# Head pairs' scores alternate in four of eight chunks, the gate's normalisation runs in steps between expert products, and second weight blocks load into other buffers

## The chip, the cores and the metric

The program runs on one core of a Trainium2 chip, in one launch. A time is the device's time for the whole program in microseconds (us), and lower is better. The engines are named as in the profile: PE (matrix products; PEld is its loading of stationary operands), DVE (vector), ACT (scalar), POOL (GpSimd), and SP, whose queue issues every DMA of this kernel.

## What is computed

The reference is an attention in blocks, then a gated feed-forward layer, then a layer of 8 experts that every token passes, weighted by a normalised gate. Cut to what matters:

```python
for c in range(768 // 32):                      # 4 x 8 heads, head size 64
    scores = scale * q_c @ k_full.T             # 32 queries, 8 memory keys + up to 56 keys around them
    a = softmax(scores); out[c] = a @ v_full
x = out.reshape(3072, 512)
x = (sigmoid(x @ w_gate) * (x @ w_val)) @ w_out # 512 -> 1536 -> 512
logits = x @ w_gate2; P = exp(logits - logits.max())       # 3072 x 8
for _ in range(8):                              # the gate's normalisation
    P /= P.sum(1, keepdims=True) + 1e-09
    P /= P.sum(0, keepdims=True) + 1e-09
    P *= N / E
out = sum(P[:, e:e+1] * (np.maximum(x @ w1[e], 0) @ w2[e]) for e in range(8))  # 512 -> 1024 -> 512
```

## The kernel before

Each large product is made of three: an operand is split into a high part (`h`) and a low part (`l`, the remainder, by `operand`, line 109: a copy on ACT, then a subtraction on POOL or DVE), and high x high, high x low and low x high are added in PSUM. Many of them are put together from seven products of half-size blocks (the names `p`, `chain`, `other`, `right`) in place of eight.

**Attention** (`attention`, line 183) works on chunks `c` of 384 tokens, 0 to 7, and on pairs of heads `hp`, 0 to 3. A pair's two heads `j` lie in partitions 0 to 63 and 64 to 127 of one tile. For each head four blocks of scores (`sc`, line 210: 64 rows of contraction, into one PSUM bank for each head), row maxima (`nm`) and exponentials with sums (line 229); chunks 0 to 3 (`PEM`) add the mask by a product on PE (line 207), chunks 4 to 7 by DVE (line 224). Then POOL scales by the sums' reciprocals, PE transposes (`pt`, line 244), and PE makes the weighted sums (`po`, line 257): four blocks for head 0 into partitions 0 to 63 of a bank, four for head 1 into 64 to 127. Outside of the first chunk all of `sc`, `pt` and `po` share two banks (`ps_a`). These products are of plain float32, and the profile records each of those of `sc` and `po` as two.

`attention` is a generator: its steps are put between the products of the feed-forward layer by a list of due places (`schedule`, `hook`). That layer runs on chunk pairs; its results go to memory (`x2d`), and the gate's logits stay on the chip.

**Experts** (the second half of `moe_chain`): the tokens go in three sets `s` of 1024, and for each set the units are (expert `e`, half `hf` of the 1024 hidden columns), each in two parts `fp`. `layer1` makes the hidden activations of a unit from `w1` (products `p`), and `layer2` the outputs from `w2` (`py` in set 0, `pzr` and `pzq` later). In set 0 the weights come raw from memory: `r1` (line 730) and `r2` (line 681), 512 KB each, both in the two buffers of tag `r` (`pair`, line 103). They are split into operands on the chip (`w1_operands`, nine tiles of tag `ws` for them; `w2_get`), and the operands are stored to memory for the later sets (`w1k`, line 144; `w2k`, lines 684 and 685). `sinkhorn` (line 608) normalises the gate `P`: in eight rounds, DVE sums and scales rows, PE sums columns by a product with ones (`pc`, line 629), DVE scales columns. Expert 0 of set 0 adds up unscaled, and is scaled by `P` when expert 1 begins (line 830).

The order of instructions is not that of the code alone. The program is written in program order, and `tile.TileContext(nc, schedule_with_timeline_sim=True)` then orders each engine's instructions when the program is built; each engine works through its own list strictly in that order. What an instruction waits for comes from the tiles that it reads and from buffers that come free.

## Time and profile before

| what | value |
|---|---|
| three runs | 2811.1, 2811.91, 2813.43 us; median 2811.91 |
| the profiled execution | 2814.29 us, its span 2812.5 us |
| PE, PEld | busy 96% and 86% of the span |
| DVE, ACT, POOL | busy 70%, 42%, 34% |
| memory | 562 MB moved, 200 GB/s on average |

The profiled execution is 2.4 us above the runs' median; the 1.8 us outside its span are start and end. A busy share is an average over very different stages: attention with the feed-forward layer reaches to about 820 us, and the first result of set 0 of the experts is stored at 1515.9 us.

### The profile page before, as it was taken

Reading aid. Unit: us, or ns where it says so; the run is one execution under the profiler, and the core shown is the slowest. Engines: PE = TensorE matmul, PEld = TensorE weight load, DVE = VectorE, ACT = ScalarE, POOL = GpSimd, SP = SyncE. Lnnn points to the kernel's source line nnn. Section 1 sums busy time; section 2 is a strip of 40 time slices with the busy share of each in tenths; the row PEclk is TensorE's granted clock in tenths of the full one; section 3 lists DMA queues with packets and bytes.
Section 4 is the critical chain, followed back from the end, with each engine's and each line's share of the span. In section 5 each row is a group of like instructions: output and inputs, shape, how many; then the busy total and the mean of one; then the engine's idle time right before and its main releaser. Section 6 shows DMA issues by size and latency. Waiting matters only on the chain.

```text
span 2812.5 us, 43343 instructions
## 1 busy us (share of the span) xinstructions
PE 2713.2 (96%) x15567; PEld 2405.6 (86%) x15567; DVE 1972.2 (70%) x3150; ACT 1189.9 (42%) x2564; POOL 970.0 (34%) x731
## 2 busy tenths in 40 slices
PE   7899999999987999999999999999998999999999
PEld 5798898999975888778877889999998899899998
DVE  8796666556576655554557798888888677667776
ACT  5565775655353333333333343433434433333332
POOL 4334774011043333333333243433434322233222
PEclk9899999999998999999999999999999999999999
DMA  5453667565654565565566566667665655555454
GB/s 201 139 177 125 241 238 244 189 201 176 204 186 169 184 213 180 176 209 177 180 207 233 178 236 220 210 225 248 239 215 184 239 192 182 203 214 214 175 183 187
DMA packets 256323, 562.04 MB, mean 200 GB/s; under 512 B 26889, under 2 KB 43785, under 8 KB 256108
## 3 DMA queue, kind: packets, MB, share of 16 engines
q1 hardware_dynamic: 256108, 559.27, 57.7%
q8 instruction: 123, 2.02, 0.3%
q14 instruction: 92, 0.75, 0.1%
HBM read 383.00 MB, written 176.16 MB: 199 GB/s over the span
## 4 chain that ended last, share of the span: by engine, by line
PE 78%; DVE 8%; DMA 5%; issue 3%; ACT 2%; POOL 2%; SPq 0%; POOLq 0%; DVEq 0%; ACTq 0%
PE p L743 9%; PE p L744 9%; PE p L745 9%; PE pzq L845 4%; PE pzq L844 4%; PE pzq L846 4%; DMA r<-in_wb 4%; PE py L76 3%; PE py L77 3%; PE py L78 3%; PE pzr L844 3%; PE pzr L845 3%; PE pzr L846 3%; PE px L77 2%; PE px L76 2%
## 5 line engine op out<-in xcount | busy, mean ns | idle before, releaser
L743 PE MATMUL p<-xh,w 128*128 128x512 f32 x1344 | 528.0, 396 | 23.4 <-ACT ce L765 12.8
L744 PE MATMUL p<-xl,w 128*128 128x512 f32 x1344 | 527.6, 393 | 0.1
L745 PE MATMUL p<-xh,w 128*128 128x512 f32 x1344 | 523.2, 392 | 1.4 <-POOL w L111 1.4
L743 PEld LDWEIGHTS p<-xh,w 128*128 128x128 f32 x1344 | 254.2, 189 | 76.6 <-ACT ce L765 19.5
L745 PEld LDWEIGHTS p<-xh,w 128*128 128x128 f32 x1344 | 253.7, 189 | 52.9 <-POOL w L111 3.1
L744 PEld LDWEIGHTS p<-xl,w 128*128 128x128 f32 x1344 | 254.4, 189 | 44.1 <-DVE xl L111 0.5
L111 POOL TENSOR_TENSOR gl<-ce,gh 128x512 fp32r<-128x512 f32 x64 | 88.2, 1378 | 545.7 <-ACT gh L110 545.7
L814 DVE SCALAR_TENSOR_TENSOR acc<-pzr,logit,acc 128x512 f32<-128x512 f32 (+1 forms) x362 | 201.0, 572 | 92.8 <-PE pzr L846 91.8
L814 DVE SCALAR_TENSOR_TENSOR acc<-pzq,logit,acc 128x512 f32<-128x512 f32 x244 | 176.7, 746 | 54.1 <-PE pzq L846 50.9
L77 PE MATMUL py<-w2b,gh 128*128 128x512 f32 x528 | 206.4, 391 | 0.0
L76 PE MATMUL py<-w2a,gh 128*128 128x512 f32 x528 | 205.9, 391 | 0.0
L78 PE MATMUL py<-w2a,gl 128*128 128x512 f32 x528 | 201.7, 391 | 0.0
L720 ACT ACTIVATE gh<-ca 128x512 fp32r<-128x512 f32 x96 | 60.6, 631 | 270.6 <-PE pzr L845 131.4
L111 POOL TENSOR_TENSOR sl<-cb,sh 128x512 fp32r<-128x512 f32 (+1 forms) x64 | 87.1, 1362 | 254.5 <-ACT sh L110 244.7
L111 POOL TENSOR_TENSOR w2b<-r,w2a 128x1024 fp32r<-128x1024 f32 x32 | 78.0, 2437 | 266.9 <-ACT w2a L110 266.9
L748 DVE TENSOR_TENSOR cd<-p,ce 128x512 f32<-128x512 f32 x96 | 65.8, 686 | 130.2 <-ACT ce L765 130.1
L844 PE MATMUL pzr<-w2c,sh 128*128 128x256 f32 x504 | 143.1, 284 | 3.7 <-DVE acc L814 3.3
L237 POOL TENSOR_TENSOR sm<-sm,rs 96x512 f32<-96x512 f32 x64 | 78.8, 1250 | 194.8 <-DVE rs L235 149.0
L845 PE MATMUL pzr<-w2d,sh 128*128 128x256 f32 x504 | 142.9, 284 | 0.0
L846 PE MATMUL pzr<-w2c,sl 128*128 128x256 f32 x504 | 141.2, 284 | 0.0
L814 DVE SCALAR_TENSOR_TENSOR acc<-py,logit,acc 128x512 f32<-128x512 f32 x116 | 84.9, 747 | 71.3 <-PE py L78 70.9
L111 POOL TENSOR_TENSOR w<-wq,w 128x512 fp32r<-128x512 f32 x64 | 87.0, 1360 | 88.5 <-ACT w L110 80.1
(288 smaller groups left out, 7824.7 us busy)
## 6 DMA issues: line engine op xcount, KB each, us to landing
w<-w1k SPq DMA_DIRECT2D x448, 256.0 KB, 4.5
w1k<-w SPq DMA_DIRECT2D x224, 256.0 KB, 4.0
r<-in_wb SPq DMA_DIRECT2D x96, 512.0 KB, 5.4
w2a<-w2k SPq DMA_DIRECT2D x64, 512.0 KB, 5.0
w2b<-w2k SPq DMA_DIRECT2D x64, 512.0 KB, 6.2
w_g<-wak SPq DMA_DIRECT2D x84, 256.0 KB, 3.5
w_v<-wak SPq DMA_DIRECT2D x84, 256.0 KB, 3.7
u<-in_qkv SPq DMA_DIRECT2D x28, 704.0 KB, 5.4
```

What stands on the lines that cost most here:

```text
L76: nc.tensor.matmul(ps, wh, xh, start=first, stop=False)
L77: nc.tensor.matmul(ps, wh, xl, start=False, stop=False)
L78: nc.tensor.matmul(ps, wl, xh, start=False, stop=last)
L111: return eng.tensor_tensor(out=l, in0=src, in1=h.bitcast(F32), op=ALU.subtract)
L237: nc.gpsimd.tensor_tensor(out=prob[j], in0=prob[j], in1=rs[:, j, :, None].to_broadcast([QB, NBLK, 128]), op=ALU.mult)
L743: nc.tensor.matmul(ps, wh[:, ks], xh, start=kk == 0 and not more, stop=False, skip_group_check=True)
L744: nc.tensor.matmul(ps, wh[:, ks], xl, start=False, stop=False, skip_group_check=True)
L745: nc.tensor.matmul(ps, wl[:, ks], xh, start=False, stop=kk == 1, skip_group_check=True)
L814: nc.vector.scalar_tensor_tensor(out=dst, in0=src, scalar=pe, in1=dst, op0=ALU.mult, op1=ALU.add)
L844: nc.tensor.matmul(ps, gh[:, cs], wh, start=fp == 0 and not more, stop=False, skip_group_check=True)
L845: nc.tensor.matmul(ps, gh[:, cs], wl, start=False, stop=False, skip_group_check=True)
L846: nc.tensor.matmul(ps, gl[:, cs], wh, start=False, stop=fp == 1, skip_group_check=True)
```

## The change

Five things are done, and each engine's list is then ordered anew:

- In chunks 4 to 7 the score products of a pair's two heads are written in turn (head 1, head 0, then 0, 1, 0, 1, 0, 1), with both banks open, and both heads' exponentials stand in one step of the generator. Chunks 0 to 3 keep their order.
- The weighted sums alternate between the heads in all chunks.
- In chunks 0 to 3 the maxima are scaled by ACT, no longer by DVE (`nm`, 32 small instructions).
- `sinkhorn` becomes a generator, moved on by every second call of `beat`, which stands ahead of each product of `layer1` and each `py` of `layer2`; what is left of it runs ahead of the third unit.
- `r2` in set 0 is no longer one block of 512 KB in a buffer of tag `r`, but two of 256 KB in buffers of tags `sh` and `sl`, which hold activations and have eight buffers each. Its copy on ACT and its subtraction on POOL are made in two halves.

```diff
--- before.py
+++ after.py
@@ -199,16 +199,27 @@
             first = c % 2
             nm = at.tile([QB, 2, NBLK], F32, tag="nm", name=f"nm{c}_{hp}")
             rs = at.tile([QB, 2, NBLK], F32, tag="rs", name=f"rs{c}_{hp}")
+            scb = [psum(f"sc{c}_{hp}_{j}")[:QB] for j in range(2)]
+
+            def score(j, b):
+                p0 = 64 * j
+                return nc.tensor.matmul(blocks(scb[j])[:, b, :], qT[p0:p0 + 64, b * QB:(b + 1) * QB],
+                                        kv[p0:p0 + 64, b, :], start=c not in PEM, stop=True, skip_group_check=c in PEM)
+
+            if c not in PEM:
+                ahead_of = score(1, 0)
+                with tc.issue_after(ahead_of.ins):
+                    score(0, 0)
+                    for b in range(1, NBLK):
+                        for j in range(2):
+                            score(j, b)
             for j in range(2):
-                p0 = 64 * j
-                scb = psum(f"sc{c}_{hp}_{j}")[:QB]
-                sc = blocks(scb)
+                sc = blocks(scb[j])
                 if c in PEM:
-                    nc.tensor.matmul(scb, mon, mro[:, first:first + NBLK].rearrange("p b q -> p (b q)"),
+                    nc.tensor.matmul(scb[j], mon, mro[:, first:first + NBLK].rearrange("p b q -> p (b q)"),
                                      start=True, stop=False, skip_group_check=True)
-                for b in range(NBLK):
-                    nc.tensor.matmul(sc[:, b, :], qT[p0:p0 + 64, b * QB:(b + 1) * QB],
-                                     kv[p0:p0 + 64, b, :], start=c not in PEM, stop=True, skip_group_check=c in PEM)
+                    for b in range(NBLK):
+                        score(j, b)
                 if lead:
                     sm = slot("v", f"sm{c}_{hp}_{j}")
                 else:
@@ -216,7 +227,7 @@
                 sm = blocks(sm[:QB])
                 if c in PEM:
                     nc.vector.tensor_reduce(out=nm[:, j], in_=sc, axis=AX.X, op=ALU.max)
-                    nc.vector.tensor_scalar(out=nm[:, j], in0=nm[:, j], scalar1=-0.125, scalar2=None, op0=ALU.mult)
+                    nc.scalar.mul(nm[:, j], nm[:, j], -0.125)
                     src, scale = sc, 0.125
                 else:
                     if not masked:
@@ -229,8 +240,10 @@
                     nc.scalar.activation(sm[:, b, :], src[:, b, :], AF.Exp, bias=nm[:, j, b:b + 1],
                                          scale=scale, accum_out=rs[:, j, b:b + 1])
                 prob.append(sm)
-                if j == 0:
+                if j == 0 and c in PEM:
                     yield
+            if c not in PEM:
+                yield
             nc.vector.tensor_scalar(out=rs, in0=rs, scalar1=1e-9, scalar2=None, op0=ALU.add)
             nc.vector.reciprocal(rs, rs)
             for j in range(2):
@@ -252,8 +265,8 @@
             yield
             po = psum(f"po{c}_{hp}")[:, 0:CT]
             pv = blocks(po)
-            for j in range(2):
-                for b in range(NBLK):
+            for b in range(NBLK):
+                for j in range(2):
                     nc.tensor.matmul(pv[64 * j:64 * j + 64, b, :], vv[:, b, j, :], pT[j][:, b, :],
                                      start=True, stop=True)
             if c < 2:
@@ -608,10 +621,12 @@
         def sinkhorn():
             m1 = sk.tile([128, 1], F32, tag="m1", name="m1")
             nc.vector.tensor_reduce(out=m1, in_=logit.rearrange("p n e -> p (n e)"), axis=AX.X, op=ALU.max)
+            yield
             pm = ps_y.tile([128, 512], F32, tag="y", name="pm")[0:1, 0:128]
             nc.tensor.transpose(pm, m1, ident)
             m2 = sk.tile([1, 1], F32, tag="m2", name="m2")
             nc.vector.tensor_reduce(out=m2, in_=pm, axis=AX.X, op=ALU.max)
+            yield
             pb = ps_y.tile([128, 512], F32, tag="y", name="pb")[:, 0:1]
             nc.tensor.matmul(pb, ones[0:1, :].to_broadcast([1, 128]), m2, start=True, stop=True)
             ng = sk.tile([128, 1], F32, tag="ng", name="ng")
@@ -625,6 +640,7 @@
                 nc.vector.tensor_tensor(out=P, in0=P, in1=r[:, :, None].to_broadcast([128, NN, E]), op=ALU.mult)
                 cs = sk.tile([128, E], F32, tag="cs", name=f"cs{i}")
                 nc.vector.tensor_reduce(out=cs, in_=P.rearrange("p n e -> p e n"), axis=AX.X, op=ALU.add)
+                yield
                 pc = ps_y.tile([128, 512], F32, tag="y", name=f"pc{i}")[:, 0:E]
                 nc.tensor.matmul(pc, ones.to_broadcast([128, 128]), cs, start=True, stop=True)
                 cr = sk.tile([128, E], F32, tag="cr", name=f"cr{i}")
@@ -632,6 +648,15 @@
                 nc.vector.reciprocal(cr, cr)
                 nc.vector.tensor_scalar(out=cr, in0=cr, scalar1=float(NT // E), scalar2=None, op0=ALU.mult)
                 nc.vector.tensor_tensor(out=P, in0=P, in1=cr[:, None, :].to_broadcast([128, NN, E]), op=ALU.mult)
+                if i % 2:
+                    yield
+
+        balance, beats = sinkhorn(), [0]
+
+        def beat():
+            beats[0] += 1
+            if beats[0] % 2:
+                next(balance, None)
 
         SW = 512
         SHB = 8
@@ -678,9 +703,10 @@
             raw = wb[e, hf, fp, :, :, 1, :]
             dh, dl = w2_tile(nm, "a"), w2_tile(nm, "b")
             if s == 0:
-                r = pair(f"r2_{nm}")
-                nc.sync.dma_start(out=r, in_=raw)
-                operand(dh, dl, nc.gpsimd, flat(r))
+                for f, k in enumerate(("sh", "sl")):
+                    r = gg.tile([128, 512], F32, tag=k, name=f"r2{k}_{nm}", bufs=SHB)
+                    nc.sync.dma_start(out=r, in_=raw[:, f, :])
+                    operand(dh[:, f * 512:(f + 1) * 512], dl[:, f * 512:(f + 1) * 512], nc.gpsimd, r)
                 nc.sync.dma_start(out=kept[0], in_=dh.bitcast(F32))
                 nc.sync.dma_start(out=kept[1], in_=dl.bitcast(F32))
                 return w2_sets(dh, dl)
@@ -737,6 +763,7 @@
                     return ps_h.tile([128, 512], F32, tag="h", name=f"p{i}_{nm}")
 
                 def product(i, ps, more=False):
+                    beat()
                     for kk in range(2):
                         ks = slice(kk * 128, (kk + 1) * 128)
                         (wh, wl), xh, xl = w[i], xop[i][0][kk], xop[i][1][kk]
@@ -820,6 +847,7 @@
 
             n_p = pairs(s, e, hf)
             for t in [h * 4 + j for j in range(n_p, 4) for h in range(2)]:
+                beat()
                 py = ps_y.tile([128, DM], F32, tag="y", name=f"py{s}_{e}_{hf}_{t}")
                 tt = slice((t % 4) * 128, (t % 4) * 128 + 128)
                 for fp in range(2):
@@ -881,7 +909,6 @@
                     each(f)
 
         xop = x_operands(0)
-        sinkhorn()
         work = [(s, e, hf) for s in range(NSB) for e in range(E) for hf in range(2)]
         gs, w2 = {}, []
         cur = layer1(0, 0, 0, xop, gs, w2)
@@ -889,6 +916,9 @@
         for n, (s, e, hf) in enumerate(work):
             for _ in cur:
                 pass
+            if n == 2:
+                for _ in balance:
+                    pass
             if e == 0 and hf == 0:
                 acc = [slot("v", f"acc{s}_{t}") for t in range(NTT)]
             args = (s, e, hf, gs, w2, acc)
```

The lists as the program is built show the following.

On PE, in chunk 7, where head pair 2's scores (`sc_2_0` for head 0, `sc_2_1` for head 1) and head pair 1's transposes stand, before:

```order
L76 MATMUL px_3_0_2_7250<-gh_3_0_0_7003,hwo_3_0_6756 128x384
L210 MATMUL sc_2_0_6910<-u_2_6906 96x128 x4
L244 MATMUL pt_1_0_6938<-ident,sm_1_0_6709 128x96 x4
...
L77 MATMUL px_3_1_1_7274<-gl_3_0_1_7085,hwo_3_0_6756 128x384
L244 MATMUL pt_1_1_6945<-ident,sm_1_1_6818 128x96 x4
L210 MATMUL sc_2_1_6968<-u_2_6906 96x128 x4
L78 MATMUL px_3_1_1_7274<-gh_3_0_1_7084,lwo_3_0_6757 128x384
```

and now:

```order
L206 MATMUL sc_2_1_6911<-u_2_6906 96x128
L206 MATMUL sc_2_0_6910<-u_2_6906 96x128 x2
L206 MATMUL sc_2_1_6911<-u_2_6906 96x128
L206 MATMUL sc_2_0_6910<-u_2_6906 96x128
L206 MATMUL sc_2_1_6911<-u_2_6906 96x128
L206 MATMUL sc_2_0_6910<-u_2_6906 96x128
L206 MATMUL sc_2_1_6911<-u_2_6906 96x128
...
L257 MATMUL pt_1_0_6950<-ident,sm_1_0_6714 128x96 x4
L257 MATMUL pt_1_1_6957<-ident,sm_1_1_6721 128x96 x4
```

Each head's run of four stood alone, with 24 products between the two runs; now the eight are one run in which the heads alternate, and the two transposes follow each other. This holds for 12 of the 16 pairs of chunks 4 to 7; in pairs 0 and 1 of chunks 4 and 6 the heads' runs still stand apart. Of the 24 groups of weighted sums in chunks 2 to 7, 13 stand as one run that alternates, and in 11 the first product stands apart from the other seven.

On SP, at the start of the experts (`r_0_0_0_1` is the second part's `r1`, then its `r2`; `w2b` is the last operand made from an `r2`), before:

```order
L684 DMA w2k_0_0_0_416<-w2a_0_0_0_9731 128x1024
L144 DMA w1k_0_0_4_196<-w_0_0_0_0_4_9635 128x512
L685 DMA w2k_0_0_1_417<-w2b_0_0_0_9732 128x1024
L731 DMA r_0_0_0_1_9739<-in_wb 128x2x512
L144 DMA w1k_0_0_5_197<-w_0_0_0_0_5_9636 128x512
L144 DMA w1k_0_0_6_198<-w_0_0_0_0_6_9637 128x512
L682 DMA r_0_0_0_1_9843<-in_wb 128x2x512
```

and now:

```order
L144 DMA w1k_0_0_5_197<-w_0_0_0_0_5_9513 128x512
L144 DMA w1k_0_1_0_199<-w_0_0_0_1_0_9654 128x512
L144 DMA w1k_0_0_6_198<-w_0_0_0_0_6_9514 128x512
L757 DMA r_0_0_1_0_9802<-in_wb 128x2x512
L144 DMA w1k_0_1_1_200<-w_0_0_0_1_1_9655 128x512
...
L144 DMA w1k_0_1_6_205<-w_0_0_0_1_6_9660 128x512
L757 DMA r_0_0_1_1_10091<-in_wb 128x2x512
...
L144 DMA w1k_1_0_4_210<-w_0_0_1_0_4_9808 128x512
L708 DMA r2sh_0_0_0_9642<-in_wb 128x512
L708 DMA r2sl_0_0_0_9646<-in_wb 128x512
```

Before, each `r1` is issued behind the store of `w2b` of the part before it, which waits for POOL; now it is issued behind the store of the last `w1` operand (`w_0_0_0_6`), four `r1` go out ahead of the first `r2`, and the `r2` are two.

On ACT, in set 0 where unit (4, 0) begins (`w` and `w2a` are copies for operands, `cb`, `ce` and `ca` empty banks of `p`), before:

```order
L759 COPY cb_3_1_1_12109<-p_0_3_1_1_12112 128x512
L110 CAST w_0_4_0_0_6_12197<-r_0_4_0_0_12189 128x256
L110 CAST w2a_4_0_1_12513<-r_0_4_0_1_12515 128x1024
L765 COPY ce_3_1_1_12110<-p_0_3_1_1_12112 128x512
L754 COPY ca_4_0_0_12218<-p_0_4_0_0_12222 128x512
```

and now:

```order
L110 CAST w_0_4_0_1_2_12483<-wq_4_0_1_12488 128x512
L746 ACTIVATE gh_3_1_1_1_12237<-cb_3_1_1_12169 128x512
L786 COPY cb_4_0_0_12283<-p_0_4_0_0_12286 128x512
L110 CAST w_0_4_0_1_4_12485<-wq_4_0_1_12488 128x512
L110 CAST w2a_3_1_1_12241<-r2sh_3_1_1_12243 128x512
L110 CAST w_0_4_0_1_6_12487<-r_0_4_0_1_12479 128x256
L110 CAST w2a_3_1_1_12241<-r2sl_3_1_1_12247 128x512
L792 COPY ce_4_0_0_12284<-p_0_4_0_0_12286 128x512
L781 COPY ca_4_0_1_12508<-p_0_4_0_1_12512 128x512
```

The copy of an `r2` still stands ahead of a `ce` on ACT, but it belongs to the unit before, and is in two parts with a `w` between. On PE, the last three `pc` stood one behind the other right ahead of the first `py`; now four of the eight stand ahead of it, 7 to 49 rows apart, and four between the `py` and `p` that follow. The last 6589 of PE's 15048 instructions, from unit (3, 0) of set 1 on, stand in the same order in both, and so do the ends of the other engines' lists.

## Rows read from the trace of the kernel before

**Rows 1.** The page's busy us, share of the span and instructions, by engine.

```profile
PE 2713.2 (96%) x15567; PEld 2405.6 (86%) x15567; DVE 1972.2 (70%) x3150; ACT 1189.9 (42%) x2564; POOL 970.0 (34%) x731
```

**Rows 2.** Windows: stretch and length, busy us (instructions) by engine, PEclk, DMA share, GB/s.

```profile
40.00:130.00 90.00, 73.92 (x403) 61.02 (x403) 79.14 (x136) 47.21 (x153) 38.20 (x26) 0.81 0.48 158
130.00:300.00 170.00, 167.07 (x1040) 152.58 (x1040) 139.50 (x240) 98.04 (x268) 71.86 (x57) 1.00 0.46 154
300.00:640.00 340.00, 333.95 (x2101) 310.84 (x2100) 215.73 (x399) 219.90 (x636) 132.86 (x128) 0.99 0.65 217
820.00:890.00 70.00, 50.65 (x207) 36.69 (x207) 58.50 (x121) 27.10 (x50) 33.47 (x23) 0.91 0.75 264
890.00:1500.00 610.00, 600.19 (x2623) 492.94 (x2624) 323.39 (x472) 209.53 (x357) 202.65 (x143) 1.00 0.53 181
```

**Rows 3.** Chain of waits, from 837 us on: start, us, what.

```profile
840.05 0.32 SPq L685
...
840.42 5.37 DMA r<-in_wb
...
853.50 5.34 DMA r<-in_wb
```

**Rows 4.** PE in order of time, 820 to 890 us: start, us, instruction, idle before.

```profile
820.12 0.50 PE L743 MATMUL p<-xh,w 128*128 128x512 f32 x1
...
880.67 0.39 PE L629 MATMUL pc<-cs,ones 128*128 128x8 f32 x2 [2.30 <-DVE cs L627]
...
884.01 0.60 PE L629 MATMUL pc<-cs,ones 128*128 128x8 f32 x2 [2.95 <-DVE cs L627]
...
889.77 0.77 PE L76 MATMUL py<-w2a,gh 128*128 128x512 f32 x1
```

**Rows 5.** PE groups by line and shape in 820 to 890 us; lines 744 and 745 alike.

```profile
L743 PE MATMUL p<-xh,w 128*128 128x512 f32 x58 | 25.0, 430 | 5.3 <-ACT w L110 4.3 <-ACT cb L759 0.8 <-ACT ce L765 0.3
```

**Rows 6.** PE in order of time, scores of one head in chunk 4.

```profile
344.69 1.11 PE L210 MATMUL sc<-u 64*96 64x128 f32 x8
345.73 0.55 PE L244 MATMUL pt<-ident,sm 96*128 96x96 f32 x4
```

**Rows 7.** PE in order of time, scores of the first chunk.

```profile
6.22 2.02 PE L210 MATMUL sc<-uk,uq 64*96 64x128 f32 x8
...
12.30 3.95 PE L210 MATMUL sc<-uk,uq 64*96 64x128 f32 x24
```

**Rows 8.** PE in order of time: a pair's weighted sums, and one head's alone.

```profile
336.00 1.26 PE L257 MATMUL po<-pT,u 128*64 128x96 f32 x16
...
455.67 0.87 PE L257 MATMUL po<-pT,u 128*64 128x96 f32 x8
```

**Rows 9.** PE in order of time: one head's scores in two runs.

```profile
462.38 0.89 PE L210 MATMUL sc<-u 64*96 64x128 f32 x6
...
464.48 0.46 PE L210 MATMUL sc<-u 64*96 64x128 f32 x2
```

**Rows 10.** Windows of line 219 alone: DVE busy us (instructions).

```profile
0.00:40.00 40.00, 5.80 (x8) 1.00 0.69 240
40.00:130.00 90.00, 4.74 (x11) 0.81 0.48 158
```

**Rows 11.** Waits in 890 to 1500 us, of PE and of ACT.

```profile
PE p L743 <- ACT ce L765: 9.8, 12, 1.6
...
ACT w2a L110 <- DMA r<-in_wb: 83.0, 14, 7.4
```

**Rows 12.** The page's DMA issues: instructions, KB each, median us to landing.

```profile
w1k<-w SPq DMA_DIRECT2D x224, 256.0 KB, 4.0
r<-in_wb SPq DMA_DIRECT2D x96, 512.0 KB, 5.4
```

**Rows 13.** All engines in order of time, 845 us: a copy for an operand on ACT.

```profile
845.87 0.62 ACT L110 CAST w<-r 128x512 fp32r<-128x512 f32 x1 [1.18 <-DMA r<-in_wb]
```

**Rows 14.** DVE's groups in 300 to 640 us: the masking that reads a score bank.

```profile
L224 DVE SCALAR_TENSOR_TENSOR sm<-sc,msk 96x512 f32<-96x512 f32 x32 | 21.9, 685 | 31.1 <-PE sc L210 30.3 <-POOL w_g L111 0.8
```

## The prediction, made before the run

> **What bounds the kernel now.** I read the page first: PE is busy for 2713 us of the span, and no engine beside it for more than 1972 [rows 1]. So time is won where PE waits, or where PE's own work shrinks. The table of windows says where it waits [rows 2]. In 130 to 640 us PE idles some 9 us of 510, and in 890 to 1500 us 10 of 610: there only less work on PE helps. In 40 to 130 us PE idles 16 us, and DVE, busy 88%, is the fullest. In 820 to 890 us PE idles 19 of 70 us, at a granted clock of 0.91, and DVE is busy 84%. The chain of waits names what ends last there [rows 3]: the store of `w2b` on SP, the load `r` issued behind it (5.4 us), operands, the next `w2b`, the next load, 13 us from load to load, while a part has 42 products for PE, less than 10 us. At the stretch's end stand three rounds of the normalisation with nothing else between them on PE, which waits 2.30 and 2.95 us for the first two of these column sums [rows 4].
>
> **Start of the experts.** The change takes both causes away: by the order on SP each `r1` leaves behind the last `w1` operand, not behind `w2b`, and four of the eight `pc` come after the first `py`. What is left for PE from its first `p` at 820.12 to its first `py` at 889.77 [rows 4]? Three lines of 58 products [rows 5] are 174; by the order, six more stand ahead of `py` now. A product costs 600.19/2623 = 0.229 us where PE hardly waits [rows 2], so 180 cost 41.2 us. Four `pc` at 0.6 are 2.4 us, and the 17 remaining instructions (logits, transposes) I put at 3. Sum 46.6: PE alone could reach `py` at 866.7. DVE cannot be ignored: of its 58.5 us [rows 2] four rounds leave, each 884.01 - 880.67 = 3.34 us [rows 4], so 45.1 remain for the same 46.6. Two engines that are both full wait for each other in turn; I take DVE at 87%, between the 82% at which PE ran without loss (130 to 300 us) and the 88% at which it lost 18% [rows 2]. That gives 51.9 us and `py` at 872.0, 17.8 earlier. The four `pc` come later (+2.4), and six products are already done (-1.4): **-16.8 us**. Bounds: -22 (PE alone), -9 (DVE at 75%). The `r2` that starts late, behind four `r1`, is hidden by these 45 us of products.
>
> **Scores.** One head's run of eight records takes PE 1.04 us, from 344.69 to the transposes at 345.73 [rows 6]. Do two heads overlap, as they use different rows of the array? Chunks 4 to 7 never show it, but the first chunk does, by chance of order: there three heads' runs follow each other, two of them a pair's. One run alone was busy for 2.02 us, and 24 records took 3.95 and not 6.06 [rows 7]. So an alternating run of 16 should cost what one of eight does, and each of the 12 pairs saves one run: 12 x 1.04 = **-12.5 us**, in stretches where PE is the bound. The transposes are as many as before. The four pairs that still stand apart gain nothing. Bounds: 0 to -12.5.
>
> Against it speaks what both heads now need at once: two banks, the only two that attention has there. Before, a bank was read out while the other head's scores waited their turn. Now PE's next transposes need both read out by DVE, 2 x 0.685 us [rows 14] with a reduction between them, about 2 us. The order puts 16 to 24 products of the feed-forward layer there, which at 167.07/1040 = 0.16 us each [rows 2] are 2.6 to 3.9 us. I take it as hidden. The Trainium skill (TensorEngine Tiling (Array Packing), Restrictions and Gotchas, Gotcha 1: PSUM Pressure) says that row tiles write to different banks and so raise the pressure on PSUM. By that rule the gain would shrink to what the two banks let through; the rival below has its price from the rows, and no row of before shows such a wait.
>
> **Weighted sums.** A pair's run of 16 records is busy 1.26 us, one head's eight 0.87 [rows 8]: the two halves overlap in part already, since the second head's first products run beside the first head's last. Alternating, the pair should cost 0.87: 13 of the 24 groups of chunks 2 to 7 save 0.39 each, **-5.1 us**. In the other 11 the first product is torn off, and a torn group costs: one head's scores in two runs were busy 0.89 + 0.46 = 1.35 [rows 9] for 1.11 in one [rows 6]. That 0.24 eats most of the 0.39; I take 0 for them. Chunks 0 and 1 lie where DVE is the bound: 0. Bounds: -9 to -2.
>
> **Maxima on ACT.** DVE spent 4.74 us on 11 such instructions in 40 to 130 us, 0.15 each when undisturbed, up to 1.2 otherwise, and 5.80 on eight in the first 40 us [rows 10]. Where they waited, the next DVE instruction may wait in their place; so I take **-3 us**, between 11 x 0.15 = 1.7 and 4.7 in the DVE-bound stretch, and nothing for the first 40 us, where the same chain (maximum, scaling, exponentials) now has its scaling on ACT. ACT is busy about half there and carries them. Bounds: 0 to -10. The order of the first 100 us changes a little everywhere, which may add or take some 3 us.
>
> **Set 0 after 890 us.** Per part, POOL and ACT get one more instruction each for the halves; both are busy a third of this stretch, and DVE and PE get nothing. There is one repeating loss: ACT, in order, waits for `r2` (83.0 us in 14 waits) [rows 11], the copy `ce` behind it comes late, and PE loses 9.8 us in 12 waits [rows 11]. Buffers of their own could bring the `r2` early. But by the new order on ACT the copies of `r2` still stand ahead of a `ce`, and their loads are issued behind `w1k` stores. So I walk through the place shown on ACT. When PE has read `w1`'s last operand of unit (3, 1), the copy `w_0_4_0_1_2` may start; 30 products of 0.229 us (6.9 us) later PE needs `w2a` of that unit. In between: the copy 0.62 [rows 13], two issues on SP of about 0.4 (840.05 to 840.42, rows 3), the half's landing, a copy 0.62. A store of the same 256 KB lands in 4.0 us, a whole `r` in 5.4 [rows 12]. With 4.0 the sum is 6.0, with 5.4 it is 7.4, late by 0.5 us. I take 0 for this stretch; bounds -10 (the old waits vanish) to +16 (16 units, about 1 us each at both parts' halves).
>
> **The sum**: -16.8 - 12.5 - 5.1 - 3 = -37.4. The profiled execution before took 2814.29 us, 1.8 of them outside its span; it becomes 2776.9. It stood 2.4 us above the median of the runs shown, so the median becomes 2774.5: 2775 us, 1.3% faster. From unit (3, 0) of set 1 on the order is the same, so nothing changes there; at the border of the sets a few us may move.
>
> **Rivals.**
>
> *The banks bind.* PE waits at each alternating pair for both read-outs, 2 x 0.685 us, 12 times 1.4 = 16 us; this eats the scores' gain: 2791. For it: two banks in all. Against: the products between.
>
> *DVE binds the start.* `py` comes at 880, and gain there is 8 instead of 17: 2784. For it: 45 us of DVE work in 46.
>
> *Better.* The waits for `ce` vanish as well (-9.8) or the maxima pay in the first 40 us: 2765.
>
> *Late `w2`, the other side.* With one half copied after the other, and behind `w` copies on ACT, each part's `py` waits for `r2`. At 1 us late per part, 32 parts, it costs 32 us: 2807, no gain left. It makes the kernel slower than before from 1.3 us late per part on (37.4 and 5.6 us over 32 parts), that is when a half lands in 6.2 us. For it: the slack of under 1 us in the walk. Against: only one of a unit's two parts stands so tight; the other has 78 products between.
>
> *The alternation does not overlap* where operands come from this order (first two products swapped): scores and sums give nothing, 2792.
>
> **How the numbers follow.** Chances: the forecast (2767 to 2783) 0.52; DVE binds 0.12; banks bind or no overlap 0.12; better 0.14; late `w2` 0.10, of which 0.04 ends slower than before. The likeliest is 2775. The range from 2758 to 2795 takes in all but the late `w2` and the far ends. A measurement of this kernel tells a difference of about 0.2%, 5.6 us, from none. Faster by more than that: 0.92; within it 0.04; slower 0.04.
>
> **What would show it.** Right, if the first `py` starts near 851 us (872 less the 20.6 won before it); if alternating runs of 16 records take about 1.1 us in chunks 4 to 7, and `po` runs 0.9; if line 219's work is gone from DVE in 40 to 130 us and PE's idle time there is less; if `r` no longer stands in the chain at the start of the experts. Wrong, if PE waits at `pt` for DVE's masking, at `pc` for `cs` as long as before, or at `py` for `w2a` and `w2b` in set 0.

## The result and the profile after

The changed kernel takes 2776.29 us (median of 4 runs, 2775.49 to 2778.06), the kernel before beside it 2811.66 us (4 runs, 2811.1 to 2813.43). The ratio is 0.9874, with a 95% interval of 0.9857 to 0.9891: 35.4 us or 1.3% faster, where 2775 us was forecast. The profiled execution took 2776.39 us, its span 2774.6 us. The sum was right; two of its terms were not, by nearly the same amount in opposite directions, and that they cancelled is luck. The table takes the same instructions in both traces as marks.

| stretch | before, us | after, us | difference | forecast |
|---|---|---|---|---|
| start to the first `p` | 820.12 | 809.29 | -10.8 | -20.6 |
| first `p` to the first `py` | 69.65 | 50.62 | -19.0 | -17.8 |
| first `py` to the 6589th instruction of PE from its end | 874.00 | 864.90 | -9.1 | +1.0 |
| from there to PE's last instruction | 1044.68 | 1045.85 | +1.2 | 0 |

The page's busy line of the changed kernel:

```profile
PE 2687.4 (97%) x15567; PEld 2385.6 (86%) x15567; DVE 1967.2 (71%) x3118; ACT 1204.0 (43%) x2628; POOL 974.1 (35%) x763
```

PE is busy for 26 us less than in [rows 1], with as many instructions. About 17 of them are the overlap (12 runs of scores at 1.03 us, 13 groups of sums at 0.38); of the rest 4.6 lie between the first `p` and the first `py`, where the same 174 `p` ran at a granted clock of 1.00 and not 0.91. The windows of the changed kernel, with the columns of [rows 2]:

```profile
40.00:130.00 90.00, 71.82 (x417) 60.89 (x417) 78.87 (x127) 51.35 (x167) 37.39 (x26) 0.84 0.47 157
130.00:300.00 170.00, 165.15 (x1046) 149.26 (x1045) 142.95 (x229) 101.44 (x287) 76.86 (x65) 1.00 0.47 164
300.00:640.00 340.00, 326.36 (x2129) 302.41 (x2127) 229.34 (x412) 221.10 (x640) 129.74 (x122) 0.98 0.64 219
820.00:890.00 70.00, 63.33 (x277) 49.52 (x276) 57.95 (x124) 32.72 (x58) 27.38 (x23) 1.00 0.59 200
890.00:1500.00 610.00, 603.88 (x2652) 497.86 (x2651) 321.14 (x499) 221.15 (x395) 212.95 (x181) 1.00 0.58 199
```

Beside [rows 2] the two late stretches lose less: 6.7 us idle in place of 19, and 6.1 in place of 9.8. The first loses more, 18.2 us in place of 16.1. The one from 300 to 640 loses more: 13.6 us idle in place of 6, at a granted clock of 0.98, and DVE is busy for 13.6 us more with 13 instructions more, which at 0.55 us each would be 7. This row is the first sign of what went wrong.

PE in order of time in the changed kernel: a pair's scores, a torn group of weighted sums, a whole one, then the start of the experts.

```profile
282.49 0.88 PE L270 MATMUL po<-pT,u 128*64 128x96 f32 x16 [1.17 <-DVE pT L263]
344.90 1.12 PE L206 MATMUL sc<-u 64*96 64x128 f32 x16
397.81 0.38 PE L270 MATMUL po<-pT,u 128*64 128x96 f32 x2
399.73 0.88 PE L270 MATMUL po<-pT,u 128*64 128x96 f32 x14
...
846.57 0.39 PE L645 MATMUL pc<-cs,ones 128*128 128x8 f32 x2 [1.16 <-DVE cs L642]
859.91 0.48 PE L76 MATMUL py<-w2a,gh 128*128 128x512 f32 x1
864.79 0.39 PE L645 MATMUL pc<-cs,ones 128*128 128x8 f32 x2 [1.91 <-DVE cs L642]
```

Sixteen alternating score records take 1.12 us, as one head's eight did (1.11, [rows 6]). A whole alternating group of sums takes 0.88 where it was 1.26 [rows 8]; a torn one takes 0.38 + 0.88 and gains nothing. The first `py` starts 30 us earlier, at 859.91 us; the prediction's sign was 851, and the 9 us between them were lost ahead of the first `p`.

PE's waits in 890 to 1500 us of the changed kernel (total, times, longest):

```profile
PE p L770 <- DVE cb L775: 3.5, 2, 2.2
PE py L76 <- ACT w2a L110: 2.4, 2, 2.2
```

The twelve waits for `ce` of [rows 11] are gone.

### The profile page after: what moved, and what is told of

Read it like the earlier page. It is cut to its first block, busy times and chain, and to the rows that moved or that the text cites. A ratio compares the mean times of both kernels' runs of the same rounds, so it can differ in the third digit from the quotient of the medians.

```text
span 2774.6 us, 43490 instructions
## 1 busy us (share of the span) xinstructions
PE 2687.4 (97%) x15567; PEld 2385.6 (86%) x15567; DVE 1967.2 (71%) x3118; ACT 1204.0 (43%) x2628; POOL 974.1 (35%) x763
## 4 chain that ended last, share of the span: by engine, by line
PE 80%; DVE 10%; DMA 3%; issue 3%; ACT 2%; POOL 1%; SPq 0%; DVEq 0%; POOLq 0%; ACTq 0%
PE p L770 10%; PE p L771 10%; PE p L772 10%; PE pzq L873 4%; PE pzq L872 4%; PE py L77 4%; PE pzq L874 4%; PE py L78 4%; PE py L76 4%; PE pzr L873 3%; PE pzr L872 3%; PE pzr L874 3%; PE px L76 2%; PE px L77 2%; PE px L78 2%
## 5 line engine op out<-in xcount | busy, mean ns | idle before, releaser
L76 PE MATMUL py<-w2a,gh 128*128 128x512 f32 x528 | 197.3, 391 | 2.4 <-ACT w2a L110 2.4
L111 POOL TENSOR_TENSOR w<-r,w 128x512 fp32r<-128x512 f32 x64 | 67.5, 1056 | 223.2 <-ACT w L110 209.3
```

The lines of the kernel that those rows point to most:

```text
L76: nc.tensor.matmul(ps, wh, xh, start=first, stop=False)
L111: return eng.tensor_tensor(out=l, in0=src, in1=h.bitcast(F32), op=ALU.subtract)
```

## The experiments

Medians and ratios are against runs of the kernel before on the same chip. "Middle" is the time from the first `p_g` to the first `p` (529.6 us before, 528.3 after). "Long" counts DVE instructions of over 1.6 us that start between 290 and 640 us, and their sum; of the changed kernel's 423 there, 388 take 0.15 to 0.69 us. Before there are 3 (7.4 us), after 10 (25.0 us). PE's waits in the middle are its gaps of over 0.15 us: 17.7 us before, 25.0 after. A stretch is read from one profiled execution, and that lay between 6.2 us below (the sums alone) and 4.2 above (all sums held together) the median of its kernel's runs, so a few us in one stretch of one kernel prove little by themselves.

### Each part alone on the kernel before

**The normalisation in steps.**

```diff
-        sinkhorn()
...
+        balance, beats = sinkhorn(), [0]
...
                 def product(i, ps, more=False):
+                    beat()
```

> The kernel before with only the normalisation in steps; the raw second blocks still share the two buffers. Theory (two causes that add): PE's last three waits for column sums ahead of the first py, 2.30 + 2.95 + 4.71 = 10.0 us, go, the loads 13 us apart stay; the first py comes 9 to 11 us earlier, after 890 us nothing changes: -10 us in all. Rival (one cause, the load chain): the last products of the second unit end at 878 whatever the rounds do, and PE waits for w operands instead: first py about 885, -4 us. Second rival (the steps alone do it, and with them the waits for the emptied banks in set 0 go too): -25 us.

Measured: 2796.51 us, ratio 0.9934 (0.9922 to 0.9946). The stretch from `p` to `py` fell from 69.65 to 46.61 us, but with 138 `p` in it in place of 174; the 36 that come later are worth 8.2 us at 0.229 each, so the gain is 14.8. The waits for `ce` stayed (8.4 us, 12 times). The direction of the theory held; the size was more than its 10. The rival of one load chain, with 4 us, falls, and so does the second one, whose waits for `ce` were to go.

**The raw second blocks in halves.**

```diff
-                r = pair(f"r2_{nm}")
+                for f, k in enumerate(("sh", "sl")):
+                    r = gg.tile([128, 512], F32, tag=k, name=f"r2{k}_{nm}", bufs=SHB)
```

> The kernel before with only the raw second blocks in halves in the activations' buffers; the normalisation still stands whole ahead of the first unit. Theory: the first py gains 5 to 8 us (products no longer wait on the load chain, but eight rounds of DVE work remain ahead of py), and the 9.8 us of PE's waits for the emptied banks ce in 890 to 1500 go, since the r2 are in early: -14 us in all. Rival (the waits for ce went because of the steps of the normalisation or a changed order, not because of the buffers): those waits stay near 10 us, and the total is -6. Second rival: the copy in two halves makes py wait: no gain or slower.

Measured: 2800.55 us, ratio 0.9944 (0.9932 to 0.9956). From `p` to `py` it gained 1.0 us, where the theory had 5 to 8: PE waits 15.1 us for column sums. From the first `py` to the mark it gained 19.2 us, in a profiled execution 5.4 us below the median. From the waits of this kernel in 890 to 1500 us, those of ACT for the halves and those of PE:

```profile
ACT w2a L110 <- DMA r2sh<-in_wb: 28.9, 18, 3.1
ACT w2a L110 <- DMA r2sl<-in_wb: 15.3, 23, 1.8
PE pc L629 <- DVE cs L627: 3.0, 1, 3.0
```

No `ce` is left, with none of the steps in the kernel, so the buffers took those waits away. ACT waits 44 us for the blocks, not 83 [rows 11], and 3.1 us at the longest, not 7.4.

**The scores alternating.**

```diff
+            if c not in PEM:
+                ahead_of = score(1, 0)
+                with tc.issue_after(ahead_of.ins):
+                    score(0, 0)
+                    for b in range(1, NBLK):
+                        for j in range(2):
+                            score(j, b)
...
```

> The kernel before with only the scores of chunks 4 to 7 alternating and both heads in one step. Theory 1 (the waits that came with it are its own: PE is through the attention earlier and stands at the feed-forward layer's boundaries, where gh, gl and x2l come from ACT and DVE): PE's busy time in 300 to 800 us falls by about 14 us as in the changed kernel, idle before px, pl and pt rises by 8 to 12, net -3 to -6 us. Theory 2 (the scores pay in full alone, and it was the other edits that took it back): net -11 to -13 us, idle in 300 to 800 us about 9 us as before.

Measured: 2807.6 us, ratio 0.9976 (0.9965 to 0.9986). The middle became 526.9 us, 2.8 less. By start-to-start times in it, `sc` fell from 33.6 to 24.0 us, waits included, and `po` rose from 19.5 to 23.8, since the new order sets the sums of 16 heads apart (two such groups of eight are busy for 0.87 us each, a joint one for 1.26 [rows 8]). Long: 8 (19.7 us). So the scores alone give back most of what they win, as theory 1 says in sum; but PE's waits in the middle rose only to 21.4 us, 3.7 more and not its 8 to 12. The rest went to the torn sums and to feed-forward products that took 3.0 us longer.

**The sums alternating.**

```diff
-            for j in range(2):
-                for b in range(NBLK):
+            for b in range(NBLK):
+                for j in range(2):
```

> The kernel before with only the weighted sums alternating. By the term of the prediction: whole groups of 16 take 0.92 us in place of 1.30, torn ones gain nothing: -5 us. By theory 1 (time won on PE inside the attention stage is given back at boundaries of the feed-forward layer): busy -2 to -4 us, idle up by as much, within 2 us of no change.

Measured: 2807.59 us, ratio 0.9976 (0.9966 to 0.9986). In the middle `po` fell from 19.5 to 13.3 us: all groups but one are whole, at 0.88, and the middle falls with it, to 523.4. The prediction's price holds, and the total, some 7 us by the ratio, is about as much.

### Where the middle's gain went

In the changed kernel PE's longest wait in the middle is before a `px` at 383.74 us. PE there, before and after the wait:

```profile
378.31 0.33 PE L76 MATMUL px<-gh,hwo 128*128 128x384 f32 x1
378.49 0.33 PE L77 MATMUL px<-gl,hwo 128*128 128x384 f32 x1
...
383.74 0.69 PE L76 MATMUL px<-gh,hwo 128*128 128x384 f32 x1 [3.88 <-DVE cvb L504]
384.22 0.52 PE L77 MATMUL px<-gl,hwo 128*128 128x384 f32 x1
384.54 0.52 PE L78 MATMUL px<-gh,lwo 128*128 128x384 f32 x1
```

DVE at the same place:

```profile
377.46 1.07 DVE L374 TENSOR_TENSOR cve<-cve,cge 128x384 f32<-128x384 f32 x1
378.45 4.77 DVE L111 TENSOR_TENSOR gl<-cvd,gh 128x384 fp32r<-128x384 f32 x1
383.14 0.54 DVE L504 TENSOR_TENSOR cvb<-p_v,cvb 128x384 f32<-128x384 f32 x1
383.61 0.61 DVE L111 TENSOR_TENSOR gl<-cve,gh 128x384 fp32r<-128x384 f32 x1
```

And POOL:

```profile
378.08 1.05 POOL L114 TENSOR_TENSOR wqv<-wl,wqv 128x256 f32<-128x256 f32 x1
379.09 1.27 POOL L111 TENSOR_TENSOR w_v<-wqv,w_v 128x512 fp32r<-128x512 f32 x1
380.32 1.25 POOL L111 TENSOR_TENSOR lwo<-wlo,hwo 128x512 fp32r<-128x512 f32 x1
381.54 1.25 POOL L111 TENSOR_TENSOR w_v<-wqv,w_v 128x512 fp32r<-128x512 f32 x1
382.76 1.03 POOL L111 TENSOR_TENSOR w_v<-wl,w_v 128x256 fp32r<-128x256 f32 x1
```

A subtraction of 0.55 us takes 4.77: it begins inside a POOL instruction, POOL goes on without a gap, and it ends 0.46 us into the fifth. The addition `cvb` behind it comes 4 us late, and PE waits for that. Behind the wait eight products start 0.32 us apart and not 0.18, that is at 1.2 GHz and not 2.4 for their 384 columns (the granted clock of 383.2 to 386.6 us is 0.51), which costs 1.2 us more. At 311.77 us the same happens with `x2l` (3.85 us) and a wait of 2.32 us.

Which DVE instructions are hit, in 290 to 640 us of the changed kernel (times in ns: least, median, most; first and last start):

```profile
L111 DVE TENSOR_TENSOR gl<-cva,gh x12: 548/558/3211, 306.1 to 633.8; 128x384 fp32r<-128x384 f32 x12
L111 DVE TENSOR_TENSOR x2l<-x,x2h x12: 542/554/3848, 306.5 to 506.9; 128x384 fp32r<-128x384 f32 x12
L111 DVE TENSOR_TENSOR gl<-cvd,gh x11: 542/551/4766, 317.0 to 616.4; 128x384 fp32r<-128x384 f32 x11
L504 DVE TENSOR_TENSOR cga<-p_g,cga x12: 544/557/558, 295.5 to 612.2; 128x384 f32<-128x384 f32 x12
```

Those with both operands in SBUF are; those of line 504, with one of them in PSUM, are not: of 93, 42 start while POOL works, and the longest takes 0.56 us. The ends say it more sharply: of the 43 DVE `TENSOR_TENSOR` with both operands in SBUF that begin in this stretch inside a POOL instruction, over 0.1 us before its end, 33 end 0.41 to 0.42 us after the end of a POOL instruction, that one or a later one. The Trainium skill (SBUF — State Buffer, SBUF: two separate sides) says that a DVE instruction with two inputs in SBUF and a GpSimd instruction that reads SBUF share an exclusive port pair, and that the one that starts later stands still for the other's whole instruction. The trace agrees on which are hit; on how long it goes further: here DVE stood through four POOL instructions in a row.

Four more kernels test this. **The scaling of the probabilities in chunks 4 to 7 on DVE in place of POOL:**

```diff
-                nc.gpsimd.tensor_tensor(out=prob[j], in0=prob[j], in1=rs[:, j, :, None].to_broadcast([QB, NBLK, 128]),
+                (nc.gpsimd if c in PEM else nc.vector).tensor_tensor(out=prob[j], in0=prob[j], in1=rs[:, j, :, None].to_broadcast([QB, NBLK, 128]),
                                        op=ALU.mult)
```

> The changed kernel with the scaling of the probabilities in chunks 4 to 7 on DVE, no longer on POOL: about 33 us less for POOL, some 18 more for DVE. Lock theory (the waits at gl, x2l and cvb come from DVE subtractions of two operands in SBUF that stand still while POOL works through a row of instructions without a gap): POOL's rows get shorter, DVE instructions over 1.6 us in 290 to 640 us fall from 10 to 5 or fewer, PE's waits in that stretch fall, 2 to 8 us faster than the changed kernel. Rival (PE only arrives sooner, DVE's load is what it waits for): with more work on DVE these waits grow, 3 to 8 us slower than the changed kernel.

Measured: 2770.52 us, ratio 0.9843 (0.9827 to 0.9859), against 0.9874 (0.9857 to 0.9891) for the changed kernel; it is the lowest of those that compute the reference. Middle 520.6 us, long 6 (10.2 us), one more than the lock theory asked for. PE's waits in the middle, 23.8 us for 25.0, did not grow with 32 instructions more on DVE; the rival falls. But they hardly shrank either, as the lock theory wanted: of the 7.7 us, 5.8 are the same 2388 feed-forward products (`p_g`, `p_v`, `px`), which took 435.3 us and not 441.1, their waits left out. The windows of 300 to 640 us show why, in the columns of [rows 2], the changed kernel's first:

```profile
300.00:640.00 340.00, 326.36 (x2129) 302.41 (x2127) 229.34 (x412) 221.10 (x640) 129.74 (x122) 0.98 0.64 219
300.00:640.00 340.00, 329.54 (x2182) 304.92 (x2180) 242.38 (x455) 228.66 (x658) 103.88 (x97) 1.00 0.66 224
```

By the record of the granted clock in the trace, it fell to half three times there in the changed kernel, for 3.4 us each, at 311.5, 383.2 and 471.9 us, just as PE came out of waits of 2.32, 3.88 and 1.29 us; with the scaling on DVE it did not fall at all. The same groups of DVE in this kernel:

```profile
L111 DVE TENSOR_TENSOR x2l<-x,x2h x14: 543/551/1654, 290.2 to 502.7; 128x384 fp32r<-128x384 f32 x14
L111 DVE TENSOR_TENSOR gl<-cva,gh x12: 548/558/1105, 309.6 to 627.5; 128x384 fp32r<-128x384 f32 x12
L111 DVE TENSOR_TENSOR gl<-cvd,gh x12: 546/551/1645, 316.9 to 639.2; 128x384 fp32r<-128x384 f32 x12
```

**The scaling left out in chunks 4 to 7.**

```diff
+                if c in PEM:
                     nc.gpsimd.tensor_tensor(out=prob[j], in0=prob[j], in1=rs[:, j, :, None].to_broadcast([QB, NBLK, 128]),
                                        op=ALU.mult)
```

> The changed kernel without the scaling of the probabilities in chunks 4 to 7; this leaves that part of the computation out (32 POOL instructions of 1.04 us). Lock theory: DVE instructions over 1.6 us in 290 to 640 us fall from 10 to 5 or fewer, PE's waits for gl, x2l and cvb there from 14 to under 8 us, 4 to 8 us faster than the changed kernel. Rival (PE only arrives sooner at what DVE and ACT have to do anyway): these waits stay, within 3 us of the changed kernel.

Measured: 2766.55 us, ratio 0.9832 (0.9818 to 0.9847). Middle 517.3 us, long 3 (4.9 us). By its size that is the whole gain that the scores' price promised: 529.6 less 12. But PE's waits for `gl` and `x2l` in 290 to 820 us hardly fell (5.6 and 3.9 us; 5.7 and 4.2 in the changed kernel); that for `cvb` on DVE (3.9) went. So the waits moved less than I expected while the time moved more. Of the 11 us in the middle, waits are 5.3 and the feed-forward products, at 436.1 us, 5.0. The step taken out also shortens the way from exponentials to transposes; but in the changed kernel PE waits only 0.3 us at the transposes there, so that way by itself had little to give.

**The generator's step between the heads kept.**

```diff
-                if j == 0 and c in PEM:
+                if j == 0:
                     yield
-            if c not in PEM:
-                yield
```

> The changed kernel with the step of the generator between the two heads kept in chunks 4 to 7, the scores alternating all the same: DVE's and ACT's work for the second head may again be put after other work. One-step theory (both heads' masks, maxima and exponentials in one block push the feed-forward layer's DVE work back, and so made the waits): the long DVE instructions and waits go back to what they were before, 4 to 8 us faster than the changed kernel. Lock theory: where POOL's and DVE's work meets is changed by any new order, without direction; within 4 us of the changed kernel, number of long DVE instructions anywhere from 3 to 12, and time with it.

Measured: 2779.2 us, ratio 0.988 (0.9862 to 0.9898); middle 527.7 us, long 11 (26.1 us), the same wait of 3.9 us for `cvb`. The one-step theory falls.

**All sums held together.**

```diff
...
+            lead_in = wsum(0, 1)
+            with tc.issue_after(lead_in.ins):
+                wsum(0, 0)
+                for b in range(1, NBLK):
+                    for j in range(2):
+                        wsum(b, j)
```

> The changed kernel with all weighted sums held together, as its scores are (the second head's first product, then the rest in one run). By the runs' prices, 11 torn groups of 0.415 + 0.910 = 1.325 us become 0.917 each: -4.5 us, if PE waits no more than before. By the lock theory the new order can give up to 4 us of it back or add as much; a group's price of 0.92 holds in either case.

Measured: 2786.42 us, ratio 0.9905 (0.989 to 0.992): 9 us slower than the changed kernel by the ratios. All groups of the middle are whole at 0.88, yet the middle is 529.9 us, and PE waits 33.0 us in it, where it is 25.0 in the changed kernel and 17.7 in the one before. And the order of the first 100 us has changed: the first `p_g` starts at 296.0 us, not 281.0. The price held, the whole did not.

### The start, the two parts together, another order, and a control

**The maxima scaled by DVE again.**

```diff
-                    nc.scalar.mul(nm[:, j], nm[:, j], -0.125)
+                    nc.vector.tensor_scalar(out=nm[:, j], in0=nm[:, j], scalar1=-0.125, scalar2=None, op0=ALU.mult)
```

> The changed kernel with the maxima scaled by DVE again. By the prediction's term (maxima on ACT give 3 us, all of it between 40 and 130 us): 3 us slower than the changed kernel, the first ps as early as in the changed kernel (35.7). Rival (the start is won by ACT's scaling in the first 40 us): first ps back near 41 and 5 to 7 us slower. Second rival (the start is a matter of the order that any edit throws anew): first ps anywhere from 36 to 43, total with it.

Measured: 2786.2 us, ratio 0.9906 (0.9893 to 0.992). The first `ps` starts at 36.7 us, nearly as early as in the changed kernel; the first `p_g` at 293.8. Neither the prediction's term nor the rival fits. The second rival fits the first `ps` but not "total with it": `ps` moved by 1.1 us and the total by 9. The loss is 11.7 us between the first `ps` and the first `p_g`, and there PE's waits are the same (22.4 us; 22.1 in the changed kernel), while the granted clock is 0.91 and not 0.94.

**Both parts of the experts, none of the attention.**

```diff
+        balance, beats = sinkhorn(), [0]
...
+                    r = gg.tile([128, 512], F32, tag=k, name=f"r2{k}_{nm}", bufs=SHB)
```

> The kernel before with both edits of the experts and none of the attention. Steps alone made the stretch from the first p to the first py 14.7 us shorter, buffers alone 1.4, and after 890 us buffers alone took 10 us of waits away. Theory (each removes a cause that the other leaves): the stretch falls by 18 to 20 us as in the changed kernel, more than 14.7 + 1.4; set 0 gains 8 to 10; -27 us in all. Rival (the two gains are the same time, won once): -15 at the start, -18 in all.

Measured: 2787.06 us, ratio 0.9911 (0.9897 to 0.9924), 26 us. From `p` to `py` 52.9 us, 16.7 less; from `py` to the mark 10.0 less. This is less than the two alone added up (18.5 and 20.2 over both stretches), and by the runs' ratios the two alone are 34 us and this kernel 25; so part of it is the same time, won once. The theory's total held, its 18 to 20 us for the stretch did not.

**Sums whole from chunk 2 on, and the scaling on DVE.**

```diff
+            if c < 2:
+                for b in range(NBLK):
+                    for j in range(2):
+                        wsum(b, j)
+            else:
+                lead_in = wsum(0, 1)
...
```

> The changed kernel with the scaling of the probabilities in chunks 4 to 7 on DVE, and the weighted sums held together from chunk 2 on, so that the first 100 us keep their order. By the runs' prices: -4.5 us against the version with the scaling on DVE alone, 2766. Rival (each new order of the attention throws the meetings of POOL and DVE anew, by several us either way): anywhere from 2762 to 2778, with the number of DVE instructions over 1.6 us in 290 to 640 us between 2 and 10.

Measured: 2771.31 us, ratio 0.9859 (0.9845 to 0.9872); long 5 (8.3 us), middle 524.4. It is no gain on the version with the scaling on DVE alone: the rival holds.

**The control: the scaling on DVE in the kernel before.**

```diff
-                nc.gpsimd.tensor_tensor(out=prob[j], in0=prob[j], in1=rs[:, j, :, None].to_broadcast([QB, NBLK, 128]),
+                (nc.gpsimd if c in PEM else nc.vector).tensor_tensor(out=prob[j], in0=prob[j], in1=rs[:, j, :, None].to_broadcast([QB, NBLK, 128]),
```

> Control: the kernel before with only the scaling of the probabilities in chunks 4 to 7 on DVE. Before, only three DVE instructions over 1.6 us (7.4 us) stood in 290 to 640 us. If the gain of 6 us that this edit had on the changed kernel came from the stalls that the alternation had brought in, there is little to gain here: within 3 us of before. Rival (less work on POOL pays whatever the order, by earlier operands): 5 to 8 us faster than before.

Measured: 2812.19 us, ratio 1.0 (0.9991 to 1.0009); middle 529.8, long 5 (8.3 us) where there were 3. Where few stalls were, the edit gives nothing. That fits the lock theory and speaks against a gain from less POOL work in any order; it does not exclude one that needs the alternating order for another reason.

## Why the prediction was right in sum

**Scores and sums: priced rightly, collected only in small part.** The run of sixteen at the price of eight held in all 12 pairs; by start-to-start times `sc` cost 33.6 us in the middle before and 21.7 after, 11.9 less for 12.5 forecast. The step that failed is "in stretches where PE is the bound": the middle became only 1.3 us shorter. PE's waits in it rose by 7.3 us, from 17.7 to 25.0, and its 2388 feed-forward products, the same in both kernels, took 6.0 us longer, 441.1 and not 435.1, more of them at the lower clock behind such waits. Some 2 us of the middle are the mark's: one group of sums, 0.8 us with a wait of 1.17 ahead, stands behind the first `p_g` now and stood ahead of it before. What stands behind two of the three longest waits, 3.88 and 2.32 us, is shown: DVE subtractions that stood still beside POOL. Over the kernels with alternating scores, those with 7 to 11 long DVE instructions (20 to 26 us) have a middle of 526.9 to 529.9, and those with 3 to 6 (5 to 10 us) one of 517.3 to 524.4; the latter are also the three whose POOL does not scale in chunks 4 to 7. No rival named this: the banks did not bind (the waits at transposes for DVE's masking come to 0.3 us), and the alternating runs did overlap. Of the sums, the 13 whole groups gained 0.38 each and the 11 torn ones nothing, as forecast; but only 5 of the 13 lie in the middle. How much of the loss was brought by the lock and how much by mere order stays open.

**Maxima and the first 300 us: mis-sized and misplaced.** Forecast were 3 us, between 40 and 130; the first `p_g` came 9.5 us earlier, and 5.4 of that was there at the first `ps`. Of the other 4.1, the seven whole groups of sums ahead of it are worth 2.7, and the group that now stands behind the mark 1.2. With DVE scaling again it goes, but the kernel with ACT scaling and all sums whole has none of it either (first `p_g` at 296.0). So ACT's scaling does not earn it by itself, and the order that the program happened to get has a part in it; what in this order earns it stays open.

**Start of the experts: right.** 50.6 us against 51.9 forecast. The chain of waits of the changed kernel there (columns of [rows 3]):

```profile
813.34 4.29 DMA r<-in_wb
817.74 2.60 DMA w1k<-w
820.36 0.26 DVE logit L360 x2
820.62 0.70 DVE wq L114
821.32 0.60 DVE gl L747
```

No load stands in it after 818 us; its largest part from there on is DVE's, `gl` and `wq` first, which is the DVE bound taken into the sum. DVE is busy for 46.6 of the 50.6 us, 92%, where 45.1 us and 87% had been taken. The six products that were to come in ahead of the first `py` did not: 174 `p` stand there in both traces, so 1.4 us of the forecast had no ground.

**Set 0 after 890 us: the step that failed is the walk on ACT.** It made the half land in 4.0 to 5.4 us, late by half a microsecond, and took 0. The halves landed in 4.0 and 3.7 us (medians), no wait for `ce` was left in 890 to 1500 us, and 9.1 us were won up to the mark, where 1.0 was to be lost; PE's waits are 5.9 of them (17.2 to 11.3 us). The two kernels with the buffers show that these take the waits for `ce` away, the one with the steps alone keeps them. The lower bound (-10) and the rival "better" had it. The size is less sure: the kernels with the scores or the sums alone have no edit in the experts, and are 4.4 and 5.0 us shorter in the same stretch. The buffers alone win some 10 us more there than the changed kernel; they leave PE 4.7 us of waits and not 11.3, and have no column sums in the stretch.

**The rivals and signs.** "Late `w2`" did not come: `py` waits 2.4 us for `w2a` in all. That PE would idle less in 40 to 130 us did not come either. "DVE binds the start" asked for `py` 8 us later. "No overlap" is refuted by the runs.

## What to carry to other kernels

Time taken out of PE's own work counts only while every operand is already there; before booking it, look at the engine that feeds the next boundary and at how much later it may come. A long wait can cost twice: here the products that ran slower took back nearly as much (6.0 us) as the waits (7.3). Where DVE subtracts or multiplies two operands in SBUF, keep POOL from working in long rows without a gap beside it: moving 33 us of small POOL work to DVE, the fuller engine, gave 0.3% in the changed order, with intervals that just meet, and nothing in the order before. And when every edit throws a scheduler's order anew, compare an edit's price by its own rows, and its total with several neighbours.

## What was not expected of the hardware

- A DVE subtraction of two SBUF operands (median 0.55 us) took up to 4.77 us beside POOL; with one operand in PSUM none of 93 took over 0.56. Most of those held up ended 0.41 to 0.42 us after the end of a POOL instruction.
- Float32 products of 64 rows and 128 columns overlapped fully when two heads alternated, as the prediction had read from the first chunk: 16 records in 1.12 us, 8 in 1.11.
